# A linear-attention and MLP kernel: last tile in three column parts, four stores split in two

## The chip, the cores and the metric

The kernel runs on one core of one Trainium2 chip. The metric is the time of one execution in device microseconds (us). A profiled execution also leaves a trace, from which the views below are taken. The engines are called as in the profile: PE is TensorE, DVE is VectorE, ACT is ScalarE, POOL is GpSimd and SP is SyncE; a small q behind the name means the engine's instruction queue, which issues DMAs and waits for semaphores.

## The reference

Linear attention is followed by a feed-forward layer. For each of 8 batches and 8 heads (576 positions, 64 columns):

```
kv  = k^T v                              (64 x 64 for a head)
o   = q kv
x   = o / sqrt(mean(o^2) + 1e-6) * g_norm      (over the 64 columns of a head)
```

The heads are laid beside each other, which gives rows of 512 columns, and then for each row:

```
xn  = (x - mean(x)) / sqrt(var(x) + 1e-6) * g_ln
out = x + max(xn @ w_ch1, 0) @ w_ch2           (512 -> 2048 -> 512)
```

Inputs and output are float32. The output has 8 x 576 = 4608 rows of 512 columns.

## The kernel before

The 4608 rows are cut into 36 tiles of 128 rows. A pair of batches gives nine tiles: four from each batch, and a ninth whose upper 64 rows belong to the one batch and whose lower 64 rows belong to the other. Four tiles make a block, so there are nine blocks. The last tile, 35, is such a ninth tile: it goes to two places of the output and is stored by two DMAs of 64 rows.

For each tile the attention part makes x (lines 445 to 527, in work buffers). The normalised row is turned by a DMA transpose from SP's queue (`t_turn_dma`, line 541) for tiles 12 to 35. The first feed-forward matmul (`m1_block`, line 591, matmuls of line 597) works on a whole block: 16 groups of four matmuls with 512 columns. The second one (`m2`, line 612, matmuls of line 616) works on one tile: 16 matmuls that add up in one PSUM tile, the stationary operand being a 128x128 piece of the first one's result, the moving operand the columns f0 to f1 of `w2`. `y_out` (line 620) multiplies that sum by the row's 1/std and adds x, on VectorE, and `store` (line 627) sends the result to the output. All stores are issued from SP's queue, except those of the last tile's second batch, which come from ACT's queue.

The order of all instructions is made in Python before anything runs. `add` and `add_dma` register steps with an engine, an occupation, a key and dependencies. `run_plan` then simulates the engines with these costs and takes, again and again, the step that can start first. A step of PE that is marked `main` must be among the first `LOOK` (8) of its kind. PSUM tiles named `mm` have four buffers in rotation. The buffer of x has `XB` = 18 copies, so that tile n waits for the store of tile n - 18, which `done[n]["store"]` keeps. Semaphores are put in by the framework: the DMAs issued by SP and ACT take eight semaphores in turn, and line 949, where the program ends, waits for all of them.

`plan_group` is where the change is. For the last tile (`split`) it makes the second matmul in two halves of 256 columns, each with its own PSUM tile, its own `y_out` and its own pair of stores. For every other tile it makes one group after another and, after the fourth, `y_out` over 512 columns and one store (two for a ninth tile).

Of the kernel before, what the change touches and what calls it, by code (L numbers as in the profile page):

```python
# [14 lines left out]
def kernel(  # L15
# [11 lines left out]
    nc = tc.nc  # L27
# [23 lines left out]
    BANKS = {"mm": 4, "out": 2, "kvt": 2}  # L51
    WARM_FROM = 9.0
    HALVED = (0,)

# [8 lines left out]
    def tile_rows(b, t):  # L65
        if t < 4:
            return [(slice(0, 128), b * S + t, 4, 128)]
        return [(fifth(b), b * S + 512, 1, 64)]


    TILES = []
# [22 lines left out]
    def add(eng, occ, dur, key, deps, fn, dma=None, alloc=None, main=False, lag=0.0):  # L94
        s = Step()
        s.eng, s.occ, s.dur, s.key, s.fn = eng, occ, dur, key, fn
        s.deps = [d for d in deps if d is not None]
        s.dma, s.alloc, s.main, s.frees, s.behind = dma, alloc, main, None, None
        s.start = s.done = None
        s.lag = lag  # L100
        steps.append(s)
        return s
# [76 lines left out]
    def act_cost(n):  # L179
        return n / 1400 + 0.115, n / 1400 + 0.23  # L180

    def dve_cost(n, rate=0.96, fix=0.075):
        return n / 1000 / rate + fix, n / 1000 / rate + fix + 0.085

    def add_dma(eng, key, deps, fn, nbytes, rate, occ=None, lat=None, tail=None):
        if eng == "POOL":
            s = add(eng, occ or 0.67, 0, key, deps, fn, dma=(1.0, nbytes / rate / 1e3, 0.6))
        else:
            s = add(eng, occ or 0.55, 0, key, deps, fn,
                    dma=(0.6 if lat is None else lat, nbytes / rate / 1e3,  # L190
                         0.75 if tail is None else tail))
        return s
# [99 lines left out]
    done = [dict() for _ in range(N_TILES)]  # L292
# [214 lines left out]
    def t_mean(n):  # L507
        m, i = divmod(n, 4)
        if n < N_SUM:
            if n in HALVED:  # L510
                nc.vector.tensor_scalar(
# [63 lines left out]
    def m1_fine(n, c):  # L575
        m, i = divmod(n, 4)
        if c == 0:
            st[n]["m1"] = work.tile([128, 4, 4, 128], bf16, tag="m1", name="m1", bufs=8)
        ps = psum.tile([128, 4, 128], f32, tag="mm", name="mm1_ps", bufs=BANKS["mm"])
        for d in range(4):  # L580
            for kk in range(nKm):
                nc.tensor.matmul(  # L582
                    ps[:, d, :], lhsT=w1[c][:, kk, d * 128:(d + 1) * 128],
                    rhs=blk[m]["xT"][:, kk, i * 128:(i + 1) * 128],
                    start=(kk == 0), stop=(kk == nKm - 1))
        st[n]["m1ps", c] = ps

    def m1_fine_out(n, c):
        nc.scalar.activation(st[n]["m1"][:, c, :, :], st[n]["m1ps", c], func=AF.Relu)  # L589

    def m1_block(m, g):
        c, d = divmod(g, 4)
        if d == 0:
            blk[m]["m1", c] = work.tile([128, 4, 512], bf16, tag="m1", name="m1", bufs=8)
        ps = psum.tile([128, 512], f32, tag="mm", name="mm1_ps", bufs=BANKS["mm"])
        for kk in range(nKm):
            nc.tensor.matmul(  # L597
                ps, lhsT=w1[c][:, kk, d * 128:(d + 1) * 128], rhs=blk[m]["xT"][:, kk, :],
                start=(kk == 0), stop=(kk == nKm - 1))
        blk[m]["m1ps", g] = ps  # L600

    def m1_block_out(m, g):
        c, d = divmod(g, 4)
        nc.scalar.activation(blk[m]["m1", c][:, d, :], blk[m]["m1ps", g], func=AF.Relu)  # L604
# [7 lines left out]
    def m2(n, c, f0=0, f1=Dm):  # L612
        if c == 0:
            st[n]["m2ps", f0] = psum.tile([128, f1 - f0], f32, tag="mm", name="mm2_ps", bufs=BANKS["mm"])
        for d in range(4):
            nc.tensor.matmul(  # L616
                st[n]["m2ps", f0], lhsT=m1_piece(n, c, d), rhs=w2[c][:, d, f0:f1],
                start=(c == 0 and d == 0), stop=(c == 3 and d == 3))

    def y_out(n, f0=0, f1=Dm):  # L620
        m, i = divmod(n, 4)
        x = st[n]["x"]
        nc.vector.scalar_tensor_tensor(  # L623
            x[:, f0:f1], in0=st[n]["m2ps", f0], scalar=blk[m]["rstd"][:, i, :],
            in1=x[:, f0:f1], op0=ALU.mult, op1=ALU.add)

    def store(n, b, eng, f0=0, f1=Dm):
        for p, r0, step, num in tile_rows(b, TILES[n][1]):
            eng.dma_start(
                out_flat[r0:r0 + (num - 1) * step + 1:step, f0:f1], st[n]["x"][p, f0:f1])  # L630
# [122 lines left out]
    def plan_tile(n):  # L753
# [9 lines left out]
        def cost(c, h0, h1):  # L763
            return c((h1 - h0) * D)
        halves = ((0, H // 2), (H // 2, H)) if n in HALVED else ((0, H),)

        q0 = okey[n] if n // 4 not in FINE else p - 12
        xs = []
        for h0, h1 in halves:
            hh = dict(h0=h0, h1=h1)  # L770
            w = (h1 - h0) / H
            d = [adone[0]["kv"][h0 // 4], adone[0]["qT", 0][h0 // 4]] if n in HALVED else deps
            o = add("PE", 0.23 * len(bs) * w, 0.23 * len(bs) * w + 0.2, okey[n], d,
# [56 lines left out]
    def plan_group(i, kind, a, c):  # L830
        if kind == "m1f":
            g = add("PE", 0.89, 1.1, i, done[a]["xT"] + load["w", 1, c], lambda: m1_fine(a, c),
                    alloc="mm", main=True)
            g.frees = add("ACT", *act_cost(512), i + 1, [g], lambda: m1_fine_out(a, c))
            done[a].setdefault("m1", []).append(g.frees)
            blk[a // 4]["m1done"] = g
        elif kind == "m1":
            g = add("PE", 0.864, 1.1, i, [d for j in range(4) for d in done[4 * a + j]["xT"]], lambda: m1_block(a, c),
                    alloc="mm", main=True)
            g.frees = add("ACT", *act_cost(512), i + 1, [g], lambda: m1_block_out(a, c))  # L840
            blk[a].setdefault("m1outs", []).append(g.frees)
            blk[a]["m1done"] = g
        else:
            n, m = a, a // 4
            m1s = done[n]["m1"] if m in FINE else blk[m]["m1outs"]
            split = n == N_TILES - 1
            parts = ((0, 256), (256, 512)) if split else ((0, 512),)
            if split:

                if c:  # L850
                    return
                for f0, f1 in parts:
                    g = add("PE", 1.75, 2.0, i, m1s, lambda f0=f0, f1=f1: [
                        m2(n, cc, f0, f1) for cc in range(4)], alloc="mm", main=True)
                    y = add("DVE", 0.4, 0.48, i + 2, [g, done[n]["rstd"]],
                            lambda f0=f0, f1=f1: y_out(n, f0, f1))
                    g.frees = y
                    for e, b in zip((nc.sync, nc.scalar), TILES[n][0]):
                        if e is nc.sync:
                            add_dma("SP", i + 3, [y], lambda f0=f0, f1=f1, b=b: store(  # L860
                                n, b, nc.sync, f0, f1), 65536, 300.0)
                        else:
                            add("ACT", 0.55, 2.3, i + 3, [y], lambda f0=f0, f1=f1, b=b: store(
                                n, b, nc.scalar, f0, f1))
                return
            g = add("PE", 0.864, 1.1, i, m1s[:4 * (c + 1) if m not in FINE else 4] + load["w", 2, c],
                    lambda: m2(n, c), alloc="mm" if c == 0 else None, main=True)
            g.behind = done[n].get("last")
            done[n]["last"] = g
            if c == 0:  # L870
                done[n]["acc"] = g
            if c == 3:
                y = add("DVE", 0.66, 0.75, i + 2, [g, done[n]["rstd"]], lambda: y_out(n))
                done[n]["acc"].frees = y
                for b in TILES[n][0]:
                    done[n]["store"] = add_dma("SP", i + 3, [y], lambda b=b: store(n, b, nc.sync),
                                               262144 // len(TILES[n][0]), 340.0)
        mains_made.append(g)


# [13 lines left out]
    for i, (kind, a, c) in enumerate(groups):  # L894
        if kind == "m1f":
            need_tile(a)
        elif kind == "m1":
            for j in range(4):
                need_tile(4 * a + j)
        plan_group(i, kind, a, c)  # L900
# [53 lines left out]
```

## Time and profile before

| | |
|---|---|
| median of 4 runs | 296.25 us (295.53 to 296.81) |
| profiled execution, its own time | 296.81 us |
| its span in the profile | 295.0 us |
| TensorE busy | 282.9 us, 96% |
| VectorE busy, ScalarE busy | 165.7 us, 143.1 us |
| granted TensorE clock | 1.0 |
| stores of 256 KB, issue to landing, median | 2.8 us, 32 of them |
| last tile's stores of 64 KB | SP 2.0 us, ACT 2.2 us, two of each |

The profile shows one execution. A line gives the engine, the line of the kernel, the operation and its tiles, and durations. In the timeline a line begins with its start and the time up to its end, both in us; in square brackets stand the idle time of the engine before it and what ended that. In the view of stretches a line begins with the stretch, followed by its length, the busy time and number of instructions of each engine that took part, the granted clock, and the busy share and rate of the DMA engines. The line "DMA to landing" gives, for DMAs issued in a window, the time from the issue to the last of their semaphore increments.

### The profile page before, as it was taken

How to read it: one execution, taken by the hardware profiler on the slowest of the kernel's cores; microseconds unless marked ns; L12 is line 12 of the kernel's file. 1: busy time of each engine (PE TensorE's matmuls, PEld its weight loads, DVE VectorE, ACT ScalarE, POOL GpSimd, SP SyncE). 2: the span in 40 equal slices, each digit the busy share in tenths (PEclk: the TensorE clock that was granted, in tenths of full speed). 3: DMA queues.
4: the chain of work that ended last, by engine and by line, in shares of the span. 5: the costliest groups of instructions: out<-in, count | busy, mean ns of one | idle time of the engine just before them, and what ended most of it. 6: DMA issues, size and time to landing. Idle time of an engine off the chain costs nothing.

```text
span 295.0 us, 5143 instructions
## 1 busy us (share of the span) xinstructions
PE 282.9 (96%) x2045; PEld 160.6 (54%) x2045; DVE 165.7 (56%) x359; ACT 143.1 (48%) x288; POOL 65.9 (22%) x92
## 2 busy tenths in 40 slices
PE   3989999999999999999999989999999999999994
PEld 1879955977754445444544435444554444444443
DVE  1596048669777877557755763577557755320022
ACT  3268963978847612761276127611761176016400
POOL 8973320208007115120422208020000000000000
PEclk9999999999999999999999999999999999999999
DMA  6999999649989997997399899998201310220012
GB/s 95 184 199 205 204 198 194 166 91 126 185 181 79 119 156 174 172 125 178 65 123 100 99 195 127 124 146 166 56 18 56 89 53 18 63 96 3 0 73 72
DMA packets 106652, 35.21 MB, mean 119 GB/s; under 512 B 85507, under 2 KB 102147, under 8 KB 106628
## 3 DMA queue, kind: packets, MB, share of 16 engines
q0 software_dynamic: 72608, 18.35, 65.0%
q1 hardware_dynamic: 33860, 16.39, 23.8%
q8 instruction: 16, 0.26, 0.4%
q10 hardware_dynamic: 160, 0.13, 0.2%
q14 instruction: 8, 0.07, 0.1%
HBM read 36.70 MB, written 9.44 MB: 156 GB/s over the span
## 4 chain that ended last, share of the span: by engine, by line
PE 89%; DMA 7%; DVE 1%; POOL 1%; issue 1%; ACT 0%; ACTq 0%; POOLq 0%
PE mm_ps L616 41%; PE mm_ps L597 33%; PE mm_ps L582 8%; DMA w<-in_moe_w_ch_dram 4%; PE out_ps L451 3%; PE kv_ps L428 3%; DMA vb<-in_v_dram 2%; PE xT_ps L532 1%; POOL kb L232 0%; PE qT_ps L400 0%; DVE x L623 0%; DVE x L503 0%; DVE ss L473 0%; POOL vb L232 0%; ACT sq L464 0%
## 5 line engine op out<-in xcount | busy, mean ns | idle before, releaser
L616 PE MATMUL mm_ps<-w,m 128*128 128x512 bf16 (+1 forms) x592 | 130.2, 373 | 0.0
L597 PE MATMUL mm_ps<-xT,w 128*128 128x512 bf16 x448 | 100.8, 379 | 1.2 <-DVE x L623 1.2
L604 ACT ACTIVATE m<-mm_ps 128x512 bf16<-128x512 f32 x112 | 66.8, 597 | 51.6 <-PE mm_ps L597 50.7
L616 PEld LDWEIGHTS <-m 128*128 128x128 bf16 x592 | 56.7, 98 | 59.8
L597 PEld LDWEIGHTS <-w 128*128 128x128 bf16 x448 | 43.0, 98 | 50.0 <-issue 1.6
L473 DVE TENSOR_REDUCE ss<-sq 128x8 f32<-128x512 f32 (+1 forms) x37 | 24.8, 670 | 46.5 <-ACT sq L464 46.4
L623 DVE SCALAR_TENSOR_TENSOR x<-mm_ps,rstd,x 128x512 f32<-128x512 f32 (+1 forms) x37 | 27.1, 734 | 42.2 <-PE mm_ps L616 42.1
L464 ACT ACTIVATE sq<-out_ps 128x512 f32<-128x512 f32 (+1 forms) x37 | 21.5, 584 | 50.9 <-PE out_ps L451 50.9
L582 PE MATMUL mm_ps<-xT,w 128*128 128x128 bf16 x512 | 30.9, 219 | 0.9 <-ACT xT L539 0.7
L582 PEld LDWEIGHTS <-w 128*128 128x128 bf16 x512 | 29.3, 98 | 1.9 <-issue 0.8
L525 DVE SCALAR_TENSOR_TENSOR xc<-x,mv,gl 128x512 bf16<-128x512 f32 (+1 forms) x37 | 27.1, 737 | 1.3 <-DVE mv L520 0.2
L468 DVE TENSOR_TENSOR xg<-out_ps,gn 128x512 f32<-128x512 f32 (+1 forms) x37 | 24.7, 669 | 0.3
L690 POOL COPY mark<-xT 128x1 bf16<-128x1 bf16 x15 | 5.4, 362 | 80.8 <-DMA xT<-xc 68.1
L589 ACT ACTIVATE m<-mm_ps 128x512 bf16<-128x512 f32 x32 | 18.3, 597 | 3.0 <-PE mm_ps L582 2.3
L503 DVE TENSOR_TENSOR x<-xg,inv 128x512 f32<-128x512 f32 x24 | 16.6, 692 | 0.8
L519 DVE BATCH_NORM_STATS2 stats<-x 128x6 f32<-128x512 f32 x24 | 16.6, 690 | 0.5
L477 ACT ACTIVATE rms<-ss,eps_attn 128x8 f32<-128x8 f32 (+1 forms) x37 | 11.1, 299 | 9.9 <-DVE ss L473 9.9
L451 PEld LDWEIGHTS <-qT 128*128 128x128 bf16 x160 | 11.6, 98 | 7.4 <-DVE kv_pack L443 0.3
L451 PE MATMUL out_ps<-kv_pack,qT 128*128 128x128 bf16 x160 | 14.9, 220 | 0.2 <-DVE kv_pack L443 0.2
L443 DVE CAST kv_pack<-kv_ps 64x256 bf16<-64x256 f32 (+1 forms) x18 | 7.1, 392 | 14.0 <-PE kv_ps L428 13.9
L428 PE MATMUL kv_ps<-vb,kp 128*128 128x128 bf16 (+1 forms) x144 | 11.3, 229 | 2.9 <-DMA vb<-in_v_dram 2.9
L428 PEld LDWEIGHTS <-kp 128*128 128x128 bf16 (+1 forms) x168 | 10.8, 102 | 4.2 <-DVE kp L382 2.3
(61 smaller groups left out, 171.3 us busy)
## 6 DMA issues: line engine op xcount, KB each, us to landing
out_dram<-x SPq DMA_DIRECT2D x32, 256.0 KB, 2.8
w<-in_moe_w_ch_dram POOLq DMA_DIRECT2D x8, 512.0 KB, 12.6
vb<-in_v_dram POOLq DMA_DIRECT2D x6, 512.0 KB, 9.3
kp<-in_k_dram POOLq DMA_DIRECT2D x5, 512.0 KB, 8.1
qp<-in_q_dram POOLq DMA_DIRECT2D x5, 512.0 KB, 9.8
qb<-in_q_dram POOLq DMA_DIRECT2D x2, 512.0 KB, 15.8
out_dram<-x SPq DMA_DIRECT2D x6, 128.0 KB, 6.4
qp<-in_q_dram POOLq DMA_DIRECT2D x10, 64.0 KB, 8.5
```

The lines of the kernel that those rows point to most:

```text
L428: nc.tensor.matmul(ps[:, hp, :], lhsT=kp[b % 2][p, t, 2 * hp:2 * hp + 2, :].rearrange("p h d -> p (h d)"), rhs=(v5[b % 2][:, 2 * hp:2 * hp ...
L451: nc.tensor.matmul(o3[:, hp, :], lhsT=att[b]["qT"][:, 4 * t + hp, :], rhs=kv_pack[b % 3][:, hp, :], start=(i == 0), stop=(i == len(bs) - 1))
L464: nc.scalar.activation(sq[:, h0:h1, :], st[n]["ps", h0][:, h0:h1, :], func=AF.Square)
L468: nc.vector.tensor_mul(xg[:, h0:h1, :], st[n]["ps", h0][:, h0:h1, :], gn.to_broadcast([128, h1 - h0, D]))
L473: nc.vector.tensor_reduce(ss[:, h0:h1, :], st[n]["sq"][:, h0:h1, :], axis=AX.X, op=ALU.add)
L525: nc.vector.scalar_tensor_tensor(xc[:, f0:f1], in0=st[n]["x"][:, f0:f1], scalar=blk[m]["mv"][:, i, 0:1], in1=gl[:, f0:f1], op0=ALU.subtrac ...
L582: nc.tensor.matmul(ps[:, d, :], lhsT=w1[c][:, kk, d * 128:(d + 1) * 128], rhs=blk[m]["xT"][:, kk, i * 128:(i + 1) * 128], start=(kk == 0), ...
L589: nc.scalar.activation(st[n]["m1"][:, c, :, :], st[n]["m1ps", c], func=AF.Relu)
L597: nc.tensor.matmul(ps, lhsT=w1[c][:, kk, d * 128:(d + 1) * 128], rhs=blk[m]["xT"][:, kk, :], start=(kk == 0), stop=(kk == nKm - 1))
L604: nc.scalar.activation(blk[m]["m1", c][:, d, :], blk[m]["m1ps", g], func=AF.Relu)
L616: nc.tensor.matmul(st[n]["m2ps", f0], lhsT=m1_piece(n, c, d), rhs=w2[c][:, d, f0:f1], start=(c == 0 and d == 0), stop=(c == 3 and d == 3))
L623: nc.vector.scalar_tensor_tensor(x[:, f0:f1], in0=st[n]["m2ps", f0], scalar=blk[m]["rstd"][:, i, :], in1=x[:, f0:f1], op0=ALU.mult, op1=AL ...
```

## The change

The last tile's second matmul is made in three column parts, of 256, 128 and 128 columns, each with its own PSUM tile, `y_out` and pair of stores. The costs given to the planner for a part follow its width. The stores of tiles 21, 23, 25 and 28 are each split in two by columns, 256 and 256, issued one after the other from SP's queue.

```diff
     HALVED = (0,)
+    SPLIT_STORE = (21, 23, 25, 28)
...
-            parts = ((0, 256), (256, 512)) if split else ((0, 512),)
+            parts = ((0, 256), (256, 384), (384, 512))
             if split:
...
                 for f0, f1 in parts:
-                    g = add("PE", 1.75, 2.0, i, m1s, lambda f0=f0, f1=f1: [
+                    w = (f1 - f0) / 256
+                    g = add("PE", 1.75 * w, 1.75 * w + 0.25, i, m1s, lambda f0=f0, f1=f1: [
                         m2(n, cc, f0, f1) for cc in range(4)], alloc="mm", main=True)
-                    y = add("DVE", 0.4, 0.48, i + 2, [g, done[n]["rstd"]],
+                    y = add("DVE", *dve_cost(f1 - f0), i + 2, [g, done[n]["rstd"]],
                             lambda f0=f0, f1=f1: y_out(n, f0, f1))
                     g.frees = y
                     for e, b in zip((nc.sync, nc.scalar), TILES[n][0]):
                         if e is nc.sync:
                             add_dma("SP", i + 3, [y], lambda f0=f0, f1=f1, b=b: store(
-                                n, b, nc.sync, f0, f1), 65536, 300.0)
+                                n, b, nc.sync, f0, f1), 65536 * w, 300.0)
...
                 for b in TILES[n][0]:
-                    done[n]["store"] = add_dma("SP", i + 3, [y], lambda b=b: store(n, b, nc.sync),
-                                               262144 // len(TILES[n][0]), 340.0)
+                    cols = ((0, 256), (256, 512)) if n in SPLIT_STORE else ((0, 512),)
+                    for f0, f1 in cols:
+                        done[n]["store"] = add_dma(
+                            "SP", i + 3, [y], lambda b=b, f0=f0, f1=f1: store(n, b, nc.sync, f0, f1),
+                            262144 // len(TILES[n][0]) // len(cols), 340.0)
```

## Prediction

> **What bounds the kernel now.** I read the page's first two parts and the chain first, then the chain of the last 20 us, then every record behind the last matmul, because the change touches the last tile and four stores.
>
> ```profile
> span 295.0 us, 5143 instructions
> PE 282.9 (96%) x2045; PEld 160.6 (54%) x2045; DVE 165.7 (56%) x359; ACT 143.1 (48%) x288; POOL 65.9 (22%) x92
> ...
> PE 89%; DMA 7%; DVE 1%; POOL 1%; issue 1%; ACT 0%; ACTq 0%; POOLq 0%
> ```
>
> TensorE is busy for 282.9 of 295.0 us and is 89% of the chain that ended last. From 95 us on the waits view has one wait of TensorE, 1.2 us before line 597 (the start of a block's first matmul, at 173.8). So until the last matmul a change pays only by taking TensorE work away, and this one takes none. What it can shorten is the tail. The chain of the last 20 us, then the timeline of VectorE and of the two queues from 288 us:
>
> ```profile
> 277.07 13.87 PE mm_ps L616 x80
> 290.94 0.03 issue
> 290.96 0.48 DVE x L623
> ```
>
> ```profile
> 289.22 0.48 DVE L623 SCALAR_TENSOR_TENSOR x<-mm_ps,rstd,x 128x256 f32<-128x256 f32 x1 [1.00 <-PE mm_ps L616]
> 290.96 0.48 DVE L623 SCALAR_TENSOR_TENSOR x<-mm_ps,rstd,x 128x256 f32<-128x256 f32 x1 [1.26 <-PE mm_ps L616]
> ```
>
> The last matmul ends at 290.94, y_out of the second half runs to 291.44, and its two stores are issued at 291.48 (SP 0.47 us, ACT 0.50). By the trace's landing records the SP one has landed at 293.44, the ACT one at 293.69. Then comes the end. The waits of SP's queue from 284 us, and SP's semaphore instructions between 293.65 and 294.17:
>
> ```profile
> SPq L949 <- DMA out_dram<-x: 1.7, 1, 1.7
> ```
>
> ```profile
> L949 SPq EVENT_SEMAPHORE  x8: 27/28/28, 293.7 to 294.1; - x8
> ```
>
> SP goes through the semaphores of all DMA lanes one after another. It stands 1.7 us at one of them, and eight more instructions follow from 293.709 to 294.139: 0.43 us for seven intervals, 0.061 each. The operands in the trace say which. The DMAs of SP and ACT take eight semaphores in rotation: 108, 110, 113, 114, 115, 116, 117, 118. The last ACT store has 108, the last SP store 110, and the end waits in this same order, so SP is stopped at the first of the eight and walks through seven that were met long before. After 118 a chain of barriers leads to 295.04.
>
> **The waits at the end.** The change adds four stores (one each for tiles 21, 23, 25, 28) and two (SP and ACT, for the third part): six more in a rotation of eight. The last two move from places 1 and 2 to places 7 and 8, to 117 (ACT) and 118 (SP). Semaphores 108 to 116, whose DMAs have landed by then, are passed while the last store is in flight. After the landing one interval is left in place of seven: 6 x 0.061 = 0.37 us saved. It lies wholly on the path. Bounds: nothing, if the last two don't fall there, and 0.43.
>
> **The last tile's matmuls.** Before, the second half is 16 matmuls of 128x256 at 109 ns start to start, the last one 272 ns long. Now two parts of 16 at 128x128, in all 32. The row for the pace is line 582, which also loads new weights for each 128-column matmul:
>
> ```profile
> 54.52:59.87 5.35, 5.35 (x96) 5.34 (x96) 1.00 0.25 86
> ```
>
> 96 in 5.35 us, 55.7 ns each, at granted clock 1.00; one record there lasts 219 ns. Before: 15 x 0.109 + 0.272 = 1.91 us from first start to last end. After: 31 x 0.0557 + 0.219 = 1.95. That is +0.04 us on the path. The upper bound is the weight load: 98 ns for one LDWEIGHTS, if they don't overlap here, so 31 x 0.0423 = 1.31 us more (+1.35). I take 55.7, since line 582 has the same shapes, type and one load for each matmul; line 616's loads run at one for each matmul too. The third part's PSUM buffer is the one of tile 33, whose y_out ended at 284.77, so it waits for nothing.
>
> The Trainium skill, "TensorE: Matmul & The Clock Gate", section Back-to-back issue gap, speaks against this part: in a real stream of weight loads and matmuls it gives about 81 ns for one of 128 columns. By that page's pace the part would cost 0.04 + 31 x 0.0253 = 0.82 us, an estimate, and the whole change would end slightly above before, at 296.5. Line 582 contradicts it with its 55.7 ns, and I go by the row.
>
> **The last y_out.** 128x512 lasts 0.748 us, 128x256 0.484: 1.03 ns for a column, so 128x128 should last 0.484 - 0.132 = 0.35 us. That is 0.13 us saved on the path (bounds: nothing, or half of 0.484, 0.24). The middle part's y_out runs while TensorE works on the third part: it starts near 289.95 and is done by 290.3, before the third part ends near 290.98. If VectorE were late the cost would be at most one such instruction, 0.35.
>
> **The last stores.** Rows of 512 B in place of 1024 B, still 64 rows for each queue. The dispatch to landing, first for 128 rows of 2048 B, then for the 64 rows of 1024 B of the first half:
>
> ```profile
> DMA to landing us min/median/max: 2.3/2.3/2.3
> ```
>
> ```profile
> DMA to landing us min/median/max: 2.0/2.1/2.2
> ```
>
> From 256 KB to 64 KB the landing comes 0.2 us sooner at the mean; 32 KB less should be worth 0.1 us or less. I take 0.1 saved. Bounds: 0.2 saved, the whole of that step again, and 0.2 lost, because two 64-row stores of 2048 B issued 0.55 us apart at 232.1 both took 2.4 us, and the third pair follows the second by only 0.85 us (1.75 before). Behind the middle part's stores on each queue stand the last ones: issued near 290.35, they occupy SP for 0.49 and ACT for 0.56 us, up to 290.9, and the last are wanted near 291.4. Without these 0.5 us of cover the overlap would be paid in full, at most 0.56. Each DMA also waits for the one eight places earlier in the rotation; for the last pair these are stores of tiles 32 and 33, landed by 287.1.
>
> **The four split stores.** Each adds one issue on SP, behind which the next SP instruction queues. SP's timeline at tile 21:
>
> ```profile
> 199.14 0.33 SPq L629 DMA_DIRECT2D out_dram<-x  x1
> 200.99 1.19 SPq L543 DMA_TRANSPOSE xT<-xc  x1
> ```
>
> After tile 23 it is 206.27 and 207.87, after 25 228.78 and 230.50, after 28 253.72 and the next store at 257.17. A second issue of 0.33 to 0.6 us fits into every gap (1.6 us at least, of which the first takes 0.33). The bytes stay the same. A 2 KB packet takes some 83 ns in the trace, a 1 KB one 44 to 78, so a tile's store costs at most 256 x 78 - 128 x 83 = 9 us of packet time over 16 engines, 0.6 us, in a stretch where the DMA engines are mostly idle. The transposes that follow serve blocks whose first matmul is far off: the last one for block 8 is issued at 252.1 and landed by 256.4, its block starts at 263.3. I cost these stores at nothing. Without that cover a transpose would be late by up to 0.6 us each time, 2.4 in all. The planner reuses x buffers 18 tiles later, so no later tile waits for these four, and its plan has SP free for a further 0.55 us at each of the four places, so the other instructions keep their order. POOL's queue gets nothing.
>
> **The sum.** -0.37 - 0.13 + 0.04 - 0.10 + 0 = -0.56 us, from the profiled execution's 296.81 (span 295.04 and 1.77 around it) to 296.25. That execution is the slowest of the four; on the median of 296.25 the sum gives **295.69**, 0.2% less.
>
> **The rivals.**
> 1. The rotation doesn't land as counted (the last pair stays ahead of met semaphores). Then only 0.19 us is left: 296.06. For it: the end's order depends on how lanes are handed out. Against it: the trace shows one rotation over both queues without a break, and +6 is fixed by the diff. Chance 0.08.
> 2. Slower: the 128-column matmuls of the last tile run at the pace of weight loads. Place: 289.0 to 291; price: 1.35 us in place of 0.04, so +0.75: 297.00. It decides from 74 ns for each matmul (0.04 + 31 x 0.0182 = 0.60, all that the rest saves). For it: the 98 ns of one load, nearly twice what a 128-column matmul leaves for it. Against it: line 582. Chance 0.07.
> 3. Faster than I say: the 512 B rows land 0.2 us sooner, y_out is halved (0.24) and all of 0.43 goes: -0.83, 295.42; with the scatter of the runs this can pass the bound. Chance 0.2.
>
> The forecast keeps 0.65.
>
> **How the numbers follow.** The four runs lie between 295.53 and 296.81, so a median may be off by some 0.4 us, and 0.3% (0.89 us) is about what a measurement of this kernel can tell from no change. The forecast and rival 1 lie within it; rival 3 lies at its edge and gets, with the forecast's own tail, 0.23 of faster. Rival 2 lies at the other edge and gives 0.06. The rest, 0.71, is within. The range: 295.42 less 0.4, and 296.06 with 0.4 and a part of the way to rival 2: 295.0 to 296.7.
>
> **What would show it.** Right: eight semaphore waits of SP before the landing, one after it; 128x128 matmuls of line 616 at 56 ns; a last y_out near 0.35 us; the last stores landed 2.0 to 2.2 us after issue; still one wait of TensorE behind 95 us. Wrong: a pace over 74 ns, a new wait of TensorE in the last three blocks, or seven waits behind the last landing still.

## The result and the profile after

The median of 32 runs of the changed kernel is 295.66 us, against 296.22 for 53 runs of the kernel before: ratio 0.998, 95% interval 0.997 to 0.9989. That is 0.56 us less. The profiled execution took 296.06 us, its span is 294.3 (before 296.81 and 295.0).

```profile
span 294.3 us, 5184 instructions
PE 283.4 (96%) x2061; PEld 161.3 (55%) x2061; DVE 166.1 (56%) x360; ACT 143.1 (49%) x288; POOL 65.3 (22%) x92
...
L617 PE MATMUL mm_ps<-w,m 128*128 128x512 bf16 (+2 forms) x608 | 130.3, 368 | 0.0
L598 PE MATMUL mm_ps<-xT,w 128*128 128x512 bf16 x448 | 100.8, 379 | 0.6 <-DMA xT<-xc 0.6
```

TensorE has 16 more matmuls and is as busy as before. The lines of the code have moved by one, so 617 is the second matmul and 598 the block's first; the program's end is line 954 in place of 949. Before line 598 there is still one wait after 95 us, 0.6 us in this execution.

The two spans differ by 0.79 us, but not all of that belongs to the change. I split each span at the first matmul of the last tile. What lies behind it I call the tail. The tail is 7.77 us before and 7.20 after; the other 0.21 us lie ahead of it, where the start and the wait near 174 us vary from one execution to the next. The change has not moved anything there: up to the last tile the two traces list the same instructions in the same order on TensorE, VectorE, ScalarE and GpSimd, and on SP up to the first split store.

The chain of the last 20 us, VectorE's timeline in the tail, the wait of SP's queue at the end, and SP's semaphore instructions after the last landing (between 293.20 and 293.39):

```profile
276.86 13.91 PE mm_ps L617 x96
290.77 0.03 issue
290.79 0.35 DVE x L624
```

```profile
289.01 0.48 DVE L624 SCALAR_TENSOR_TENSOR x<-mm_ps,rstd,x 128x256 f32<-128x256 f32 x1 [1.00 <-PE mm_ps L617]
289.90 0.35 DVE L624 SCALAR_TENSOR_TENSOR x<-mm_ps,rstd,x 128x128 f32<-128x128 f32 x1 [0.41 <-PE mm_ps L617]
290.79 0.35 DVE L624 SCALAR_TENSOR_TENSOR x<-mm_ps,rstd,x 128x128 f32<-128x128 f32 x1 [0.54 <-PE mm_ps L617]
```

```profile
SPq L954 <- DMA out_dram<-x: 1.2, 2, 1.0
```

```profile
L954 SPq EVENT_SEMAPHORE  x2: 28/28/28, 293.3 to 293.3; - x2
```

The tail's three parts hang together as before: the last matmul, at once the last y_out, then the stores. SP now stands at more than one semaphore (1.2 us in two waits in this view), since it reaches those of the middle pair before that has landed. Two semaphore instructions are left where eight stood; the others were passed while the last stores were in flight. The stretch of the last part shows the pace of TensorE:

```profile
289.90:290.78 0.88, 0.85 (x16) 0.68 (x13) 0.35 (x1) 0.00 (x0) 0.00 (x0) 1.00 0.09 23
```

16 matmuls in 0.88 us; their start times in the trace are 55 to 56 ns apart. The last stores and the middle ones, from issue to landing:

```profile
DMA to landing us min/median/max: 1.9/2.0/2.1
```

```profile
DMA to landing us min/median/max: 2.5/2.5/2.5
```

At the mean the last pair lands 0.1 us sooner after its issue than the last tile's pairs before (2.1 us), the middle pair 0.4 us later. Why the middle pair is late is taken up in experiments 4, 6 and 9.

### The profile page after: what moved, and what is told of

Its sections match the earlier page's. It is cut to its first block, busy times and chain, and to the rows that moved or that the text cites. A ratio compares the mean times of both kernels' runs of the same rounds, so it can differ in the third digit from the quotient of the medians.

```text
span 294.3 us, 5184 instructions
## 1 busy us (share of the span) xinstructions
PE 283.4 (96%) x2061; PEld 161.3 (55%) x2061; DVE 166.1 (56%) x360; ACT 143.1 (49%) x288; POOL 65.3 (22%) x92
## 4 chain that ended last, share of the span: by engine, by line
PE 88%; DMA 7%; POOL 3%; issue 1%; DVE 1%; ACT 0%; ACTq 0%; POOLq 0%
PE mm_ps L617 39%; PE mm_ps L598 33%; PE mm_ps L583 9%; DMA qp<-in_q_dram 4%; DMA xT<-xc 3%; PE out_ps L452 3%; PE kv_ps L429 3%; POOL qp L254 1%; PE xT_ps L533 1%; PE qT_ps L401 1%; POOL kb L233 1%; POOL w L334 1%; POOL vb L233 0%; DVE ss L474 0%; ACT sq L465 0%
## 5 line engine op out<-in xcount | busy, mean ns | idle before, releaser
L617 PE MATMUL mm_ps<-w,m 128*128 128x512 bf16 (+2 forms) x608 | 130.3, 368 | 0.0
L624 DVE SCALAR_TENSOR_TENSOR x<-mm_ps,rstd,x 128x512 f32<-128x512 f32 (+2 forms) x38 | 27.3, 721 | 41.9 <-PE mm_ps L617 41.8
L691 POOL COPY mark<-xT 128x1 bf16<-128x1 bf16 x15 | 4.6, 308 | 80.3 <-DMA xT<-xc 67.7
```

The source lines that it names most:

```text
L617: nc.tensor.matmul(st[n]["m2ps", f0], lhsT=m1_piece(n, c, d), rhs=w2[c][:, d, f0:f1], start=(c == 0 and d == 0), stop=(c == 3 and d == 3))
L624: nc.vector.scalar_tensor_tensor(x[:, f0:f1], in0=st[n]["m2ps", f0], scalar=blk[m]["rstd"][:, i, :], in1=x[:, f0:f1], op0=ALU.mult, op1=AL ...
```

## The experiments

All numbers below that are given from a run's trace have the last tile's first matmul as zero. "Landing to end" is the time from the last semaphore increment of the last stores to the end of the span. Each row is one profiled execution; how far a tail repeats can be seen from the change and experiment 10, which turned out to carry out the same stores with the same semaphores: 7.20 and 7.17. The 95% intervals of most of the times overlap, so the terms are told apart by the tails and not by the times. My theory was the sum of the prediction; the main rival was that the end costs the same wherever the last stores lie in the rotation, and that the gain is the narrower last part.

| run | column parts | split stores | last matmul ends | last ACT store issued | its landing after issue | landing to end | tail |
|---|---|---|---|---|---|---|---|
| before | 256, 256 | 0 | 3.66 | 4.21 | 2.21 | 1.35 | 7.77 |
| the change | 256, 128, 128 | 4 | 3.70 | 4.12 | 2.09 | 0.99 | 7.20 |
| 1 | 256, 128, 128 | 0 | 3.70 | 4.12 | 2.07 | 1.22 | 7.41 |
| 2 | 256, 256 | 6 | 3.66 | 4.21 | 2.22 | 0.99 | 7.42 |
| 3 | 256, 128, 128 | 6 | 3.70 | 4.12 | 2.16 | 1.35 | 7.63 |
| 4 | 384, 128 | 6 | 3.66 | 4.39 | 2.47 | 0.99 | 7.85 |
| 5 | 256, 128, 128, last two stored together | 6 | 3.70 | 4.12 | 2.22 | 0.98 | 7.32 |
| 6 | 320, 192 | 6 | 3.66 | 4.15 | 2.12 | 0.99 | 7.25 |
| 7 | 256, 192, 64 | 4 | 3.70 | 4.32 | 2.03 | 0.98 | 7.33 |
| 8 | 256, 128, 128, one store each | 7 | 3.70 | 4.11 (SP) | 6.47 | 0.93 | 11.51 |
| 9 | 384, 128, first ACT store left out | 7 | 3.66 | 4.08 | 2.10 | 0.99 | 7.17 |
| 10 | as the change | 4 | 3.70 | 4.12 | 2.06 | 0.99 | 7.17 |

**1. The column parts alone.**

> Three column parts, no split stores. Tail = from the last tile's first matmul to the end of the span; 7.77 us before, 7.20 with the change. Theory (place in the rotation counts, 0.061 us for each semaphore behind the last landing): two more DMAs in the rotation put the last pair on 113 and 114, so five intervals stay behind the landing in place of one: landing to end 0.99 + 4 x 0.061 = 1.23 us, tail 7.44, the store's own 2.1 us from issue to landing unchanged. Rival (the end costs the same wherever the last pair lies; the gain is the narrower last part): landing to end 0.99 as with the change, tail 7.20.

```diff
-    SPLIT_STORE = (21, 23, 25, 28)
+    SPLIT_STORE = ()
```

SP's semaphore instructions after the last landing:

```profile
L954 SPq EVENT_SEMAPHORE  x6: 28/28/28, 292.5 to 292.8; - x6
```

Six instead of two, landing to end 1.22 us (expected 1.23), tail 7.41. Ratio to before 0.999 (0.9979 to 1.0001). The rival's 0.99 is ruled out.

**2. The split stores alone.**

> Two halves as before, six split stores (tiles 21, 23, 25, 28, 29, 30) so that the last pair again gets 117 and 118. Theory: landing to end 0.99 us as with the change, last y_out 0.48, ACT store 2.21 us to landing as before, tail 7.77 - 0.36 = 7.41. Rival (the gain is the narrower last part): tail 7.77. Rival (split stores cost time in the middle): a wait of TensorE after 195 us and a span up to 0.6 us longer for each of the six.

```diff
-    SPLIT_STORE = (21, 23, 25, 28)
+    SPLIT_STORE = (21, 23, 25, 28, 29, 30)
...
-            parts = ((0, 256), (256, 384), (384, 512))
+            parts = ((0, 256), (256, 512))
```

Landing to end 0.99, tail 7.42, as the theory had it, and TensorE has no wait after 95 us at all. Ratio 0.9989 (0.9968 to 1.0009). In this execution six split stores cost nothing on the path.

**3. All of the change, and the rotation made round.**

> Three column parts and six split stores: eight more DMAs than before, so the rotation is round and the last pair is back on 108 and 110, with every other part of the change kept. Theory: seven intervals behind the landing, landing to end 1.35 us, tail 7.20 + 0.37 = 7.56. Rival: 7.20.

```diff
-    SPLIT_STORE = (21, 23, 25, 28)
+    SPLIT_STORE = (21, 23, 25, 28, 29, 30)
```

```profile
L954 SPq EVENT_SEMAPHORE  x8: 28/28/28, 293.4 to 293.8; - x8
```

With two further split stores all eight instructions are back behind the landing, and the end takes 1.35 us as before. Nothing else of the change was undone. The tail is 7.63; 0.36 of the 0.43 us above the change are the end, the other 0.07 are a store that landed 2.16 us after its issue. The ratio is 1.0 (0.9989 to 1.0012): with its last stores at the wrong place of the rotation, the change as a whole is not seen in the time.

**4. Two parts, the last one narrow.**

> Two column parts of 384 and 128, six split stores, so again 117 and 118. Asks whether the middle pair of stores holds the last one up. Theory (it does not): last matmul ends 3.66 us after the first one (16 x 0.163 + 15 x 0.056 + 0.219; 3.70 with the change), y_out 0.35, ACT store 2.09 us to landing, tail 7.16. Rival (the 512 B stores queue behind the middle pair, whose own landing took 2.46): the last stores land 0.2 to 0.4 us sooner after their issue, tail 6.8 to 7.0.

```diff
-    SPLIT_STORE = (21, 23, 25, 28)
+    SPLIT_STORE = (21, 23, 25, 28, 29, 30)
...
-            parts = ((0, 256), (256, 384), (384, 512))
+            parts = ((0, 384), (384, 512))
```

Both theories were wrong. TensorE and VectorE did what was expected, but the last pair landed later, not sooner:

```profile
L630 ACTq DMA_DIRECT2D out_dram<-x x2: 478/520/561, 289.8 to 290.7; - x2
L630 SPq DMA_DIRECT2D out_dram<-x x1: 497/497/497, 290.4 to 290.4; - x1
...
DMA to landing us min/median/max: 2.5/2.6/2.6
```

ACT issued its last store at 4.39, 0.3 us behind SP's. Its first one had ended at 4.01 and the data was ready at 4.04; with the change, too, ACT's second issue starts 0.37 us after the end of its first (3.40 after 3.03). The runs don't show why. Both last stores took 2.5 to 2.6 us; the view's line counts ACT's first store as well. The landing records show 15 of ACT's 16 increments between 6.07 and 6.26 and the 16th at 6.86; for SP's store 15 up to 6.06 and one at 6.69. So one of the 16 increments was late. At 5.54 the trace has one packet of 8 KB on the queue that the page calls q14, instruction, 0.35 us long. In the run of the change a packet like that lies at 4.28 and lasts 0.63 us, and there it is the middle pair that has 15 increments in time and one 0.6 us behind. This gave a new theory: that packet holds up whatever store is on its DMA engine. The packets of the stores in the traces bear it out. SP's middle store in the run of the change has 64 packets; 60 of them start between 4.35 and 4.63, the last four, one sixteenth, only from 4.91 on, when the 8 KB packet ends (4.91). In this experiment 60 of the last store's start up to 5.57 and four from 5.89 on, where the 8 KB packet ends (5.89). Experiments 1, 3 and 10 show the same for their middle pair: in all five runs the four late packets of SP's store begin within 4 ns of that end. Ratio 1.0006 (0.9991 to 1.0021).

**5. The third part's matmuls and y_out, without narrow rows.**

> Matmuls and y_out in the three parts of the change, but no stores of the middle part: the last pair carries columns 256 to 511, rows of 1024 B, after the third y_out. Six split stores, so again 117 and 118. Separates the rows' width from the rest. Theory (narrower rows land 0.13 us sooner): ACT store 2.21 us from issue to landing as before, issue 4.12 us after the last tile's first matmul as with the change, tail 4.12 + 2.21 + 0.99 = 7.32. Rival (the width of the rows does not matter): landing 2.09, tail 7.20.

```diff
                     g.frees = y
+                    if f0 == 256:
+                        continue
+                    if f0 == 384:
+                        f0 = 256
```

(The split stores are those of experiment 4.) Stores of 1024 B rows land 2.22 us after issue, tail 7.32. By these two runs the rows' width is worth 0.13 us (2.22 against 2.09); this run leaves out the middle pair too, so it changes more than the width. Over all runs, without the stores that an instruction packet met, ACT's stores of 64 rows landed 2.21 to 2.25 us after issue with 1024 B, 2.12 to 2.13 with 768, 2.06 to 2.16 with 512 and 2.03 with 256. Ratio 0.9986 (0.9971 to 1.0001).

**6. Two parts, further apart.**

> Two column parts of 320 and 192, six split stores. In the run with 384 and 128 the last pair landed 2.5 to 2.6 us after its issue, with one of the 16 semaphore increments 0.6 us behind the other 15, while one 8 KB packet of the instruction queue ran in those 0.4 us; with the change such a packet fell on the middle pair. Theory (a DMA engine that fetches instructions holds up the one store in flight on it): the first pair is issued near 3.02, the fetch follows 1.25 to 1.6 us later, by 5.0 at the latest, and is over before the last pair's packets begin near 5.3; so landing 2.1 to 2.2, last y_out 0.42, tail 7.25 to 7.30. Rival (a pair of narrow stores less than 0.9 us behind another pair lands late whatever is fetched): landing 2.4 to 2.6, tail 7.5 to 7.7.

```diff
-            parts = ((0, 256), (256, 384), (384, 512))
+            parts = ((0, 320), (320, 512))
```

(The split stores are those of experiment 4.) The instruction packet ran from 4.81 to 5.26, ahead of the last pair, which landed 1.9 and 2.1 us after its issue:

```profile
DMA to landing us min/median/max: 1.9/2.0/2.1
```

The tail is 7.25, so this fits the theory; but the pair was also 1.19 us behind the first, not 0.63, so it doesn't rule out the rival. Ratio 0.997 (0.9954 to 0.9987), which cannot be told from the change's 0.998.

**7. A last part of 64 columns.**

> Column parts of 256, 192 and 64, four split stores as with the change. Asks where the weight loads set the pace, which the third way of the prediction feared for 128 columns. Theory (one load for each 55.7 ns at best, so a 64-column matmul is no faster than a 128-column one): the 16 narrow matmuls run at 50 to 56 ns, last matmul ends near 4.1 us after the first, y_out 0.29, tail 7.4 to 7.6. Rival (pace follows the columns, some 29 ns): last matmul ends at 3.70, tail 7.1.

```diff
-            parts = ((0, 256), (256, 384), (384, 512))
+            parts = ((0, 256), (256, 448), (448, 512))
```

```profile
L617 PE MATMUL mm_ps<-w,m 128*128 128x64 bf16 x16 | 0.6, 193 | 0.0
...
L624 DVE SCALAR_TENSOR_TENSOR x<-mm_ps,rstd,x 128x64 f32<-128x64 f32 x1 | 0.3, 284 | 0.0
```

(What the expectation calls the third way of the prediction is its rival 2.) My theory of the pace was wrong and the rival's pace right: 16 matmuls of 64 columns take 0.6 us, the starts are 28 to 30 ns apart, and each has its own weights. The last matmul ends at 3.70 as with 128 columns. The rival's tail of 7.1 did not come; it is 7.33: the middle pair, issued at 3.71 and 3.72, occupies SP until 4.19 and ACT until 4.22, and the last stores go out at 4.28 and 4.32, while y_out was done at 4.02. The 0.07 us saved on VectorE are more than lost on the queues: ACT's last store goes out 0.20 us later than with the change. The execution's span of 295.9 us is long for a reason ahead of the tail, a wait of TensorE of 1.8 us near 175 us. Ratio 0.9996 (0.9978 to 1.0013).

**8. One store for both batches.**

> Three column parts, but each part's two stores (SP and ACT, 64 rows each) are one store of 128 rows from SP; seven split stores (19, 20, 21, 23, 25, 28, 29), so that the last one gets 118. Theory: nothing is left to pass behind the last landing, landing to end 0.99 - 0.06 = 0.93 us; the one store lands as late as the later of two, 2.1 us after an issue at 4.11; tail 7.14. If ACT's instruction queue asked for the 8 KB fetch, none is seen at 4.3 us. Rival (128 rows on one queue take longer than 64 on each of two, as the 128 rows of 2048 B with 2.3 us): landing 2.3, tail 7.35.

```diff
-                    for e, b in zip((nc.sync, nc.scalar), TILES[n][0]):
...
+                    add_dma("SP", i + 3, [y], lambda f0=f0, f1=f1: nc.sync.dma_start(
+                        out[6:8, 512:576, f0:f1], st[n]["x"][:, f0:f1]), 131072 * w, 300.0)
```

(Seven split stores: 19, 20, 21, 23, 25, 28, 29.) Neither the 2.1 us nor the 2.3 us of the expectation came: the three stores landed 5.1, 5.9 and 6.5 us after issue, the later ones behind the packets of those before; ratio 1.0118 (1.0092 to 1.0145). Their semaphores show three increments where the others show 16: one within 1.0 us of the issue and two at the end. So each store ran on two DMA engines, one for each batch, for 128 packets of 1024 B or 512 B. The Trainium skill says so in "DMA: Bandwidth & Descriptors", section Why a DMA increments its semaphore by 16 and not by 1: the number of engines is the largest up to 16 that divides the size of the slowest dimension on both sides, here 2 by the output's, and the issuer writes the remaining increments at once. The trace agrees, with its three records. Two of my guesses held: the landing to the end took 0.93 us with the last store on 118, and without a store from ACT there was no instruction packet at 4.3 us.

**9. Experiment 4 without its first store from ACT.**

> Two column parts of 384 and 128 as in the run where the last pair landed 2.5 to 2.6 us after issue, but the first part's store from ACT is left out (64 rows by 384 columns of the output are not written); seven split stores, so the last pair again has 117 and 118. Theory (ACT's store issue is what makes an 8 KB instruction fetch come 1.25 to 1.6 us later; that fetch held the last pair up): no fetch between 4.0 and 5.9 us behind the last tile's first matmul; SP store 1.9 and ACT store 2.1 us from issue to landing, no increment far behind the others; tail 4.08 + 2.1 + 0.99 = 7.15 to 7.2. Rival (two stores of one queue 0.6 us apart hold each other up): SP store still 2.5 us or more, tail 7.5 or more.

```diff
-                        else:
+                        elif f0:
```

(Parts of 384 and 128, and the split stores of experiment 8.) The last pair, from issue to landing:

```profile
DMA to landing us min/median/max: 1.8/2.0/2.1
```

SP's stores follow each other by 0.63 us as in experiment 4, yet the last ones take 1.8 and 2.1 us, all 16 increments of each lie within 0.23 us, and the instruction packet comes only at 6.33. One time, 296.19 us, was taken. The tail is 7.17. So two SP stores at this distance do not hold each other up, and the packet comes after ACT's first store issue. (The left-out store's own packets are gone too, so the run alone doesn't part the two; the four late packets under experiment 4 do.)

**10. SP's store ahead of ACT's in the order.**

> The change as it is, with SP's store ahead of ACT's in the order that hands out semaphores, so that ACT's last store, which lands last, has 118 and SP's has 117. Theory: nothing is left to pass behind the last landing, landing to end 0.99 - 0.06 = 0.93 us, tail 7.13, the best of all; in the time, 0.06 us less than with the change, too little to see. Rival (the end's remaining cost doesn't hang on the order): 0.99 and 7.20.

```diff
-        order.sort(key=lambda s: s.start)
+        order.sort(key=lambda s: (s.start, s in late))
```

(`late` holds ACT's store steps.) The edit did not reach its aim: ACT's last store still has 117 and SP's 118, so a sort that only parts steps with equal start isn't what decides it. The run repeats the change: tail 7.17, landing to end 0.99, ratio 0.9987 (0.9974 to 1.0001). Whether the last 0.06 us can be had in this way stays open; experiment 8 alone shows 0.93.

## Why the prediction was right

The forecast was 0.56 us less by a sum of five terms. The tails of the two profiled executions differ by 0.575 us, and the medians by 0.56. That the medians meet the forecast to the hundredth is luck: by the interval of the ratio the gain lies between 0.33 and 0.89 us. What bears the prediction out is that the terms were found one by one:

| term | predicted | measured | shown by |
|---|---|---|---|
| waits behind the last landing | -0.37 | -0.36 | experiments 1 to 3: 1.22, 0.99 and 1.35 us from landing to end |
| matmuls of the last tile | +0.04 | +0.04 | last matmul ends at 3.70 in place of 3.66 |
| last y_out | -0.13 | -0.13 | 0.351 us in place of 0.484 |
| narrower last stores | -0.10 | -0.13 | 2.09 us in place of 2.21; experiment 5 with 2.22 |
| four split stores | 0 | 0 on the path | no wait of TensorE behind them in any run; experiment 2 with six |

**The waits** are the largest term, and experiment 3 is the direct proof: the same change with two more stores gives them back. With the 1.22 of experiment 1 the four steps from one to five intervals are worth 0.23 us, 0.058 each, near the predicted 0.061. Rival 1 is ruled out.

**The pace of TensorE.** Rival 2 is ruled out: the 128-column matmuls ran at 55 to 56 ns, as line 582 had said. Experiment 7 goes further: even 64 columns run at 29 ns with a weight load for each. The 81 ns that the Trainium skill gives ("TensorE: Matmul & The Clock Gate", Back-to-back issue gap) are not seen in the last tile of any of these runs.

**The last stores.** A pair can land late by more than the 0.2 us that I allowed, but it was the middle pair (2.5 us) and not the last. The distance to the pair before, which I named as the cause, is not it: at 0.63 us SP's store took 2.6 us in experiment 4 and 1.8 in experiment 9. What fits all the runs is the instruction packet on one DMA engine. The views don't say which engine a packet ran on; that it is one is inferred from 15 increments in time and one late, and from the four of 64 packets that begin as the instruction packet ends. The change escapes it because its last pair is issued 1.65 us after the first, and the packet at 4.28 is over by 4.91, before the last pair's packets begin near 5.2. The prediction knew nothing of this packet, so this escape was luck; experiment 4, whose last pair met it, has a tail of 7.85. The 0.5 us of cover behind the middle pair's issue were 0.24 us on ACT, whose middle store went out 0.18 us behind SP's.

**The split stores.** I put a second issue at 0.33 to 0.6 us. Two of the four took 0.42, but those of tiles 25 and 28 took 1.23 and 1.26 us:

```profile
228.57 1.62 SPq L630 DMA_DIRECT2D out_dram<-x  x2
230.35 1.19 SPq L544 DMA_TRANSPOSE xT<-xc  x1
```

So the length of a second issue was mis-sized by a factor of two or more at two of the four places. The gap up to the transpose did not quite cover it either: the transpose behind tile 25 starts 1.78 us after the first issue, against 1.72 before, and 1.88 in experiment 8, where the second issue took 1.33. That this cost nothing is seen from TensorE, which waits nowhere behind it.

The traces also show what the long ones have in common. A 16 KB packet of the queue that the page calls q8, instruction, ran from 228.74 to 229.81 and from 253.82 to 254.81 us, and the two issues ended 0.37 us behind it. In the change and experiments 2 to 10 all 20 second issues of tiles 25 and 28 overlap such a packet, take 0.68 to 1.53 us and end 0.33 to 0.40 us after it; of the 36 that meet none, 34 take 0.42 us and two, of tile 20, 0.64. That the second issue waits for the packet fits all of them, but no run varied it.

Rival 3 asked for -0.83 us and did not come: no term reached its far bound. As to the wait of TensorE near 174 us, the profiled executions show from none to 1.8 us; it lies ahead of all edits of the change, in an order of instructions that is the same as before, and adds scatter.

Three readings of the prediction were off without touching the sum. The matmul behind that wait starts at 175.3 us, not 173.8. The stores eight places ahead of the last pair are those of tiles 31 and 32, landed by 283.5, not of 32 and 33. A 1 KB packet of the last tile's stores before takes up to 92 ns, not 78.

## What to carry to other kernels

When a program ends by going through its DMA semaphores in a fixed order, the store that lands last should have the last one: each semaphore behind it costs some 0.06 us on the path. Count the DMAs modulo the rotation, and check it by two more, which must take the gain away. A narrower last piece pays as long as its stores don't meet the issue of the piece before on the same queue (experiment 7), nor an instruction packet (experiment 4).

## What the runs showed of the hardware that I had not expected

- An instruction packet of 8 KB took 0.3 to 0.6 us in the tails and, by what five runs suggest, holds back one engine's share of a store: four of 64 packets start when it ends, and the last increment comes 0.4 to 0.7 us behind the other 15 (15 up to 6.26, the 16th at 6.86). It followed the first store issue on ACT's queue: 4.28 with a first ACT issue at 2.47, 5.54 with 3.45, 6.33 with 4.08, and none before the program's end without one.
- Matmuls with a weight load each keep pace with their columns down to 64: 109 ns for 256, 82 to 83 for 192, 56 for 128, 29 for 64, at granted clock 1.0.
- A store issue on SP directly behind another took 0.42 us, but 0.68 to 1.53 at the 20 places where a 16 KB instruction packet ran, ending 0.33 to 0.40 us after that packet.
- A store whose outer dimension is 2 ran on two DMA engines: 5.1 us to landing for 128 KB, against 2.0 and 2.2 for two stores of 64 KB.
